# Attention products in four 32-column groups: shapes of the TensorE array, four reciprocals, and a planner that keeps two engines apart

## The chip, the core and the metric

The kernel runs on one core of a Trainium2 chip. Five engines work side by side there: TensorE (PE in the profile; its weight loads are PEld), VectorE (DVE), ScalarE (ACT), GpSimd (POOL) and SyncE (SP), which issues the transfers. Each works through its own list of instructions in order and waits on semaphores for the others. The metric is the device time of one execution in microseconds (us), as the median of several runs. Before the change it is 1353.37 us, the median of 3 runs (1352.94 to 1354.53).

## The reference

Three layers follow each other. The first is a linear attention over 4 batches, 8 heads, 576 positions of 64 numbers, with 128 features:

```python
def phi(x):
    proj = np.einsum('bhsd,df->bhsf', x, w_phi)
    proj = proj - np.max(np.abs(proj), axis=-1, keepdims=True)
    return np.concatenate([np.exp(proj), np.exp(-proj)], axis=-1)
q_p, k_p = (phi(q), phi(k))
kv = np.einsum('bhsf,bhsd->bhfd', k_p, v)
z = np.sum(k_p, axis=2)
num = np.einsum('bhsf,bhfd->bhsd', q_p, kv)
den = np.einsum('bhsf,bhf->bhs', q_p, z)[..., None] + 1e-06
return (num / den).astype(np.float32)
```

Its output, as 2304 tokens of 512 numbers, goes through a feed-forward layer (`x @ w_in`, a leaky activation with a slope for each of 2048 channels, `@ w_out`), and then through four experts of 1024 channels, whose outputs are added with normalised weights.

## The kernel before

Two heads make a pair, so there are 16 pairs. For each pair the attention stage does the following steps. Their names are those of the planner's operations, and the lines are those of the kernel before.

- `P` (L349) projects the keys, then the queries, into five PSUM banks that are handed out in turn (`bank`). A product has 64 rows, so two heads run in two row groups of the array. `PT` (L356) projects the last 64 positions.
- `R` and `S` (L365, L371) on DVE take the largest magnitude and subtract it. `E` and `X` on ACT make the exponentials.
- `KV` (L392) multiplies values and exponentials of the keys: weights of 64 columns, two heads in two column groups. `ZZ` (L401) sums the keys by products with ones, in four column groups of 32. `Z` (L413) adds halves of the keys ahead of it, on DVE or POOL.
- `TV` (L425, L427) turns the result, `T` (L440, L437) transposes the shifted queries.
- `A` (L458, function `attend`) makes the numerators: weights of 64 columns, one column group for each head, with the two halves of the positions in two calls (c = 0, 1). `AD` (L468, `denominators`) makes the denominators in four column groups of 32, one for each head and half.
- `I` (L479 to L486, `invert`) on DVE turns the denominators over, takes eight reciprocals of 32 partitions and spreads them out. `X0`, `X1`, `X2` multiply, round, and take the rest, which gives the feed-forward layer its input in two parts (`Xh`, `Xl`).

Beside it the first feed-forward weights are unpacked (`W`, steps L195 to L201 on DVE, L588 and L595 on DVE or POOL), and blocks of 12 feed-forward products (`U`, L239; `M`, L260) are put between the pairs. When the stage is done, the second stage (the rest of the feed-forward layer) and the experts follow in the order in which they are written.

A product's groups of rows and columns set the shape of the array: row groups (`row`), two column groups (`col`), four column groups (`quarter`), or the whole array (`full`, and `rounded` for the feed-forward products).

Inside the attention stage the order is that of a planner, the class `Plan`. It knows the cost of each operation on each engine that may do it, what must be done before, and how many buffers a ring has. Step by step it picks the operation that can begin first. Among those that begin alike, the lower rank goes first: a number from the table `RANK` plus the pair's number, with `STAY` added where PE would have to change its shape. Each engine then runs its list in that order.

Of the kernel before, what the change touches and what calls it, by code (L numbers as in the profile page):

```python
# [19 lines left out]
P = 128  # L20
B, H, S, D, F = 4, 8, 576, 64, 128
NP = H // 2
NT = B * S
DM = H * D
# [25 lines left out]
RANK = dict(  # L50
    ld=14.86, Pt=-7.2, PT=-11.04, Pk=-11.49, Pq=-3.94, E=17.62, Z=-30.21, KV=-2.39, TV=-18.36, Q=-14.5,
    A=-0.06, F=16.1, W=40.35, U=12.87, G=4.84,
)
# [5 lines left out]
class Plan:  # L59
# [7 lines left out]
    SWITCH = 100  # L67
    STAY = 0.57

    def __init__(self):  # L70
        self.ops, self.bufs, self.readers, self.begun, self.modes = {}, {}, {}, set(), {}

    def op(self, name, costs, after, rank, emit, alloc=(), reads=(), behind=(), late=0, mode=None):
        self.ops[name] = (costs, after, rank, emit, alloc, {*after, *behind}, late)
        self.modes[name] = mode
        for x in reads:
            self.readers.setdefault(x, []).append(name)

    def run(self):
# [23 lines left out]
        def turn(name, e):  # L103
            return self.SWITCH if e == "t" and self.modes[name] != mode[0] else 0

        while ready:
            found = []
            for name in ready:
                t = room(name)
                if t < np.inf:  # L110
                    costs, rank = self.ops[name][0], self.ops[name][2]
                    begin = lambda e: max(t, free.get(e, self.START))
                    e = min(costs, key=lambda e: begin(e) + costs[e] + BIAS.get(e, 0))
                    found.append((begin(e), rank + self.STAY * (turn(name, e) > 0), order[name], name, e))
# [35 lines left out]
def fused(ctx: ExitStack, tc: tile.TileContext, qT, kT, v_main, v_tail, w_phi, alpha, probs, w64, wup, wdn, out):  # L150
# [134 lines left out]
    with ExitStack() as st1:  # L285
# [164 lines left out]
        def attend(p, c):  # L450
# [4 lines left out]
            for s in range(2):  # L455
                for h in range(2):
                    r = slice(h * D, (h + 1) * D)
                    nc.tensor.matmul(nd[r, :HS], tl["kvt", p][:, s * P + h * D:s * P + (h + 1) * D],  # L458
                                     tl["qe", p][:, h, s, c * HS:(c + 1) * HS], start=s == 0, stop=s == 1,
                                     tile_position=(0, h * D), skip_group_check=True)  # L460

        def denominators(p):
            nd = new("bank", ("d", p))
            for s in range(2):
                for h in range(2):
                    for c in range(2):
                        r = 32 * (2 * h + c)
                        nc.tensor.matmul(nd[r:r + 32, :HS], tl["kvt", p][:, 2 * P + s * D + h * 32:2 * P + s * D + (h + 1) * 32],  # L468
# [6 lines left out]
        def invert(p):  # L475
# [24 lines left out]
        for p in range(len(pairs)):  # L500
            for n in "kq":
# [4 lines left out]
            op(("PT", p), {"t": pe32(F, 2)}, [("ld", n, p) for n in "kq"], RANK["PT"] + p, alloc=[("bank", ("t", p))],  # L506
               reads=[(n + "r", p) for n in "kq"], mode="col", emit=lambda e, p=p: project_tails(p))
            for key in [(n, p, h) for n in "kq" for h in range(2)] + [("t", p)]:
# [7 lines left out]
            for h in range(2):  # L516
# [5 lines left out]
            kes = [("ke", (p, h)) for h in range(2)]  # L522
            op(("KV", p, 0), {"t": pe32(2 * F, 2)}, [*es, ("ld", "v", p)], RANK["KV"] + p, alloc=[("kv", p)], mode="col",
               emit=lambda e, p=p: key_values(p, 0))
            op(("KV", p, 1), {"t": pe32(2 * F, 3)}, [("KV", p, 0), ("E", p, 2)], RANK["KV"] + p + 0.1, reads=[*kes, ("ket", p), ("v", p), ("vt", p)],
               mode="col", emit=lambda e, p=p: key_values(p, 1))
            zs = []
            if p >= NZ:
                zs = [("Z", p, h) for h in range(2)]
                for h in range(2):  # L530
                    op(("Z", p, h), lo_cost(512), [("E", p, h)], RANK["Z"] + p, alloc=[("zsum", (p, h))],
                       reads=[("ke", (p, h))], emit=lambda e, a=(p, h): sum_keys(*a, e))
# [19 lines left out]
            for c in range(2):  # L552
                pr_ = RANK["A"] + p + 0.1 * c
                op(("A", p, c), {"t": pe32(HS, 2)}, [*xs[:2 + c], ("VH", p)], pr_, reads=[("qe", p), ("kvt", p)], behind=[("A", p, 0)] * c,
                   alloc=[("bank", ("n", p, c))] + [("num", p)] * (c == 0), mode="col",
                   emit=lambda e, a=(p, c): attend(*a))
# [4 lines left out]
            pr_ = RANK["F"] + p  # L561
            op(("I", p), {"v": 370 + 200 + 8 * 80 + 700}, [("AD", p)], pr_, alloc=[("di", p), ("dt", p), ("dj", p), ("rb", p)],
               reads=[("bank", ("d", p)), ("dt", p), ("di", p), ("dj", p)], emit=lambda e, p=p: invert(p))
            op(("X0", p), lo_cost(S), [("I", p)] + [("N", p, c) for c in range(2)], pr_, reads=[("rb", p)],
               emit=lambda e, p=p: x_part(p, 0, e))
            op(("X1", p), hi_cost(S), [("X0", p)], pr_, emit=lambda e, p=p: x_part(p, 1, e))
            op(("X2", p), lo_cost(S), [("X1", p)], pr_, reads=[("num", p)], emit=lambda e, p=p: x_part(p, 2, e))

# [29 lines left out]
        for i, (c, half) in enumerate(early):  # L598
# [5 lines left out]
            for k, cost in costs.items():  # L604
                op(("W", k, c, half), cost, before, RANK["W"] + WSTEP * i,
                   alloc=[("area", i)] * (k == 0), reads=[("area", i)] * (k == 5), late=4200 * (k == 0),
# [18 lines left out]
        for blk in range(NA):  # L625
            tok = sum(BLOCKS[blk])
            have = [("X2", p) for p, (b, j) in enumerate(pairs) if b * S < tok]
            for cs in (tuple(range(GRP)),):
                for c in cs:
# [7 lines left out]
                       emit=lambda e, a=g: g_step(*a, 0, e))  # L637
                    op(("G1", *g), hi_cost(BLK), [("G0", *g)], pr_, emit=lambda e, a=g: g_step(*a, 1, e))
                    op(("G2", *g), lo_cost(BLK), [("G1", *g)], pr_, alloc=[("gl", g)], reads=[("t", g)],
                       emit=lambda e, a=g: g_step(*a, 2, e))  # L640
# [352 lines left out]
```

## Time and profile before

| What | Value |
|---|---|
| Median of 3 runs | 1353.37 us |
| The profiled execution | 1352.19 us |
| Its span in the trace | 1350.2 us |
| PE busy in the span | 1331.8 us (99%), 7616 matmul records |
| DVE busy | 776.5 us (58%) |
| ACT busy | 443.3 us (33%) |
| POOL busy | 256.9 us (19%) |

The attention stage, with the planner's order, takes about the first 270 us of the span. A product of 32-bit numbers shows as two records, so the four products of one call of `attend` are eight records. Records of PE overlap in the profile, and their ends are modelled. Time on PE is therefore read from start to start here.

### The profile page before, as it was taken

The page shows a single profiled execution, that of the slowest core. Times are in us where ns is not written, and L with a number is a line of the kernel's source. Part 1 is how long each engine was busy: PE and PEld are TensorE (multiplying, and loading weights), DVE is VectorE, ACT ScalarE, POOL GpSimd, SP SyncE. Part 2 cuts the span into 40 slices and gives each one's busy share as a digit, 9 for nine tenths or more (in the row PEclk, how much of TensorE's full clock was granted, in tenths as well). Part 3 has the DMA queues.
Part 4 walks back from the last instruction along what each step waited for, and adds up shares of the span by engine and source line. Part 5 has one row for each costly group of instructions (what it writes and reads, how often), then busy time and mean ns, then how long its engine had stood idle before and what let it go on. Part 6 is the DMA issues. An engine that isn't in the chain of part 4 may idle for free.

```text
span 1350.2 us, 20101 instructions
## 1 busy us (share of the span) xinstructions
PE 1331.8 (99%) x7616; PEld 1130.8 (84%) x7616; DVE 776.5 (58%) x1365; ACT 443.3 (33%) x943; POOL 256.9 (19%) x268
## 2 busy tenths in 40 slices
PE   8899999999999999999999999999999999999998
PEld 5566667788888888898899998998999998899997
DVE  7898766699779555665455446443333363343332
ACT  5655654233122121144444443222222232222221
POOL 1244323012011030056566640000000000000000
PEclk9999999999999999999999999999999999999999
DMA  5222220123102011048877755665566666555641
GB/s 179 85 86 70 63 62 11 48 94 94 48 27 68 0 62 64 0 172 293 296 262 257 252 216 181 225 194 188 188 192 194 197 221 201 172 171 181 192 142 47
DMA packets 103487, 192.27 MB, mean 142 GB/s; under 512 B 13920, under 2 KB 14048, under 8 KB 103392
## 3 DMA queue, kind: packets, MB, share of 16 engines
q1 hardware_dynamic: 103392, 191.00, 43.1%
q8 instruction: 60, 0.98, 0.3%
q14 instruction: 35, 0.29, 0.1%
HBM read 140.10 MB, written 50.86 MB: 141 GB/s over the span
## 4 chain that ended last, share of the span: by engine, by line
PE 89%; DVE 7%; DMA 2%; ACT 1%; issue 1%; SPq 0%; POOL 0%; DVEq 0%; ACTq 0%; POOLq 0%
PE dn L901 29%; PE up L854 25%; PE up L239 12%; PE dn L260 12%; PE mm L260 2%; PE kv L392 2%; PE bank L458 1%; PE bank L349 1%; DVE m L365 1%; PE bank L468 1%; DVE dj L485 1%; PE mm L239 1%; PE kv L401 1%; PE bank L440 1%; DVE pmk L371 1%
## 5 line engine op out<-in xcount | busy, mean ns | idle before, releaser
L901 PE MATMUL dn<-whd,Xh 128*128 128x512 f32 x720 | 231.4, 390 | 0.0
L912 DVE SCALAR_TENSOR_TENSOR acc<-dn,pr,acc 128x512 f32<-128x512 f32 x126 | 88.7, 749 | 190.9 <-PE dn L901 190.9
L854 PE MATMUL up<-Xl,wlu 128*128 128x384 f32 x864 | 158.6, 335 | 0.8 <-DVE c L867 0.6
L901 PEld LDWEIGHTS dn<-whd,Xh 128*128 128x128 f32 x720 | 135.1, 188 | 27.0
L867 DVE TENSOR_TENSOR c<-up,p 128x384 f32<-128x384 f32 x96 | 53.5, 557 | 174.2 <-PE up L854 174.2
L854 PEld LDWEIGHTS up<-Xl,wlu 128*128 128x128 f32 x864 | 150.3, 188 | 2.0 <-DVE c L867 1.5
L901 PE MATMUL dn<-Xh 128*128 128x512 f32 x648 | 151.8, 389 | 0.0
L901 PEld LDWEIGHTS dn<-Xh 128*128 128x128 f32 x648 | 121.6, 188 | 25.5
L901 PE MATMUL dn<-wld,Xh 128*128 128x512 f32 x360 | 140.8, 391 | 0.0
L872 ACT COPY p<-up 128x384 f32<-128x384 f32 x48 | 23.1, 481 | 326.6 <-PE up L854 326.6
L854 PE MATMUL up<-Xl,whu 128*128 128x384 f32 x576 | 111.8, 334 | 1.2 <-ACT p L872 1.2
L854 PEld LDWEIGHTS up<-Xl,whu 128*128 128x128 f32 x576 | 101.2, 188 | 1.5 <-ACT p L872 1.5
L861 ACT ACTIVATE Xh<-c 128x384 fp32r<-128x384 f32 x144 | 75.7, 526 | 79.7 <-DVE c L867 79.7
L239 PE MATMUL up<-Xl,whu 128*128 128x512 f32 (+1 forms) x272 | 99.1, 364 | 0.0
L260 PE MATMUL dn<-gh,wld 128*128 128x512 f32 (+1 forms) x272 | 99.1, 364 | 0.0
L260 PE MATMUL dn<-gh,whd 128*128 128x512 f32 (+1 forms) x272 | 99.1, 364 | 0.0
L239 PE MATMUL up<-Xh,whu 128*128 128x512 f32 (+1 forms) x272 | 99.1, 364 | 0.0
L239 PE MATMUL up<-Xh,wlu 128*128 128x512 f32 (+1 forms) x272 | 99.0, 364 | 0.0
L260 PE MATMUL dn<-gl,whd 128*128 128x512 f32 (+1 forms) x272 | 99.0, 364 | 0.0
L862 DVE SCALAR_TENSOR_TENSOR Xh<-c,Xh 128x384 fp32r<-128x384 f32 x144 | 86.1, 600 | 5.4
L184 ACT CAST gh<-t 128x512 fp32r<-128x512 f32 (+1 forms) x68 | 38.6, 569 | 147.7 <-DVE t L251 147.7
L901 PEld LDWEIGHTS dn<-wld,Xh 128*128 128x128 f32 x360 | 67.5, 188 | 13.1
(172 smaller groups left out, 2226.6 us busy)
## 6 DMA issues: line engine op xcount, KB each, us to landing
whu<-wsu SPq DMA_DIRECT2D x96, 256.0 KB, 3.4
wlu<-wsu SPq DMA_DIRECT2D x96, 256.0 KB, 3.2
st<-w SPq DMA_DIRECT2D x24, 512.0 KB, 3.4
wsu<-whu SPq DMA_DIRECT2D x48, 256.0 KB, 3.1
wsu<-wlu SPq DMA_DIRECT2D x48, 256.0 KB, 3.0
Xh<-wsd SPq DMA_DIRECT2D x48, 256.0 KB, 3.8
wld<-wsd SPq DMA_DIRECT2D x40, 256.0 KB, 3.0
whd<-wsd SPq DMA_DIRECT2D x40, 256.0 KB, 3.3
```

The lines of the kernel that those rows point to most:

```text
L184: nc.scalar.copy(hi, src)
L239: nc.tensor.matmul(ps[:, :bn], a[:, cs], x[:, cc, t0:t0 + bn], start=n == 0, stop=n == 3 * CC - 1)
L260: nc.tensor.matmul(ps, w[:, sl], g, start=start and k == 0, stop=stop and k == 2)
L349: nc.tensor.matmul(ps[h][:, i], x[r, i * P:(i + 1) * P], w0[r, h], start=True, stop=True, tile_position=(h * D, 0), skip_group_check=True)
L392: nc.tensor.matmul(kv[h * D:(h + 1) * D, 0], a, e, start=i == 0, stop=i == NM, tile_position=(0, h * D), skip_group_check=True)
L854: nc.tensor.matmul(ps[name], w[k][:, r, kt * P:(kt + 1) * P], slots[k][:, x + kt], start=start and n == 0, stop=stop and n == 5, skip_grou ...
L861: nc.scalar.activation(gh, src, AF.Relu)
L862: nc.vector.scalar_tensor_tensor(gl, src, 0.0, f32(gh), ALU.max, ALU.subtract)
L867: nc.vector.tensor_tensor(o, ps[name], x, ALU.add)
L872: nc.scalar.copy(p1, ps["pb"])
L901: nc.tensor.matmul(ps[m], x[:, sl], w, start=c == chunks[0] and k == 0, stop=c == chunks[-1] and k == 2)
L912: nc.vector.scalar_tensor_tensor(av, ps[m], pe, av, ALU.mult, ALU.add)
```

## The change

- `PT`, `KV` and `A` are cut into products of 32 columns, four groups at once. `A` and `AD` order the 128 output rows by the half of the head first and by the head second, and the rows of the feed-forward weight `w_in` are put in the same order ahead of the launch. With that order, one reciprocal serves both heads, so `invert` issues four of 64 partitions.
- The planner counts a change of shape twice where the new shape is the whole array, and none between `full` and `rounded`. It no longer lets an operation of POOL run beside one of those of DVE that are marked `port`. Its costs of a feed-forward product and of `I`, `STAY` and the table `RANK` have other values.

```diff
-    STAY = 0.57
+    STAY = 0.98
 ...
         def turn(name, e):
-            return self.SWITCH if e == "t" and self.modes[name] != mode[0] else 0
+            new, old = self.modes[name], mode[0]
+            if e != "t" or new == old or {new, old} == {"full", "rounded"}:
+                return 0
+            return self.SWITCH * (2 if new in ("full", "rounded") else 1)
...
-                    begin = lambda e: max(t, free.get(e, self.START))
+                    port = lambda e: e == "p" or e == "v" and name in self.ports
+                    begin = lambda e: max(t, free.get(e, self.START), free.get("port", 0) if port(e) else 0)
...
+            if e == "p" or e == "v" and name in self.ports:
+                free["port"] = start + cost
...
-        pe = lambda n, k=1: k * (n / 2.4 + 3)
+        pe = lambda n, k=1: k * (n / 2.4 + 13)
...
-                for h in range(2):
-                    nc.tensor.matmul(ps[h * TL:(h + 1) * TL, i * F:(i + 1) * F], tl[n + "r", p][:, NM * P:], w0[:, h],
-                                     start=True, stop=True, tile_position=(0, h * TL), skip_group_check=True)
+                for o in range(0, P, 32):
+                    nc.tensor.matmul(ps[o:o + 32, i * F:(i + 1) * F], tl[n + "r", p][:, NM * P + o % TL:NM * P + o % TL + 32], w0[:, o // TL],
+                                     start=True, stop=True, tile_position=(0, o), skip_group_check=True)
...
-                    nc.tensor.matmul(kv[h * D:(h + 1) * D, 0], a, e, start=i == 0, stop=i == NM,
-                                     tile_position=(0, h * D), skip_group_check=True)
+                    for o in range(0, D, 32):
+                        nc.tensor.matmul(kv[h * D + o:h * D + o + 32, 0], a[:, o:o + 32], e, start=i == 0, stop=i == NM,
+                                         tile_position=(0, h * D + o), skip_group_check=True)
...
-                for h in range(2):
-                    r = slice(h * D, (h + 1) * D)
-                    nc.tensor.matmul(nd[r, :HS], tl["kvt", p][:, s * P + h * D:s * P + (h + 1) * D],
+                for o in range(0, P, 32):
+                    to, h = divmod(o // 32, 2)
+                    a = s * P + h * D + to * 32
+                    nc.tensor.matmul(nd[o:o + 32, :HS], tl["kvt", p][:, a:a + 32],
                                      tl["qe", p][:, h, s, c * HS:(c + 1) * HS], start=s == 0, stop=s == 1,
-                                     tile_position=(0, h * D), skip_group_check=True)
+                                     tile_position=(0, o), skip_group_check=True)
...
-                        r = 32 * (2 * h + c)
+                        r = 32 * (2 * c + h)
...
-            for h in range(2):
-                for c in range(2):
-                    for to in range(2):
-                        a, o = (32 * (2 * h + x) for x in (c, to))
-                        nc.vector.reciprocal(dj[o:o + 32, c * n:(c + 1) * n], di[a:a + 32])
+            for c in range(2):
+                for to in range(2):
+                    nc.vector.reciprocal(dj[to * D:(to + 1) * D, c * n:(c + 1) * n], di[c * D:(c + 1) * D])
...
-    w64 = a(np.stack(chunks(moe_w_in, moe_w_out), axis=1)).view(np.int64)
+    rows = moe_w_in.reshape(CC, 2, 2, 32, DFF).transpose(0, 2, 1, 3, 4).reshape(DM, DFF)
+    w64 = a(np.stack(chunks(rows, moe_w_out), axis=1)).view(np.int64)
```

The operations marked `port` are `Z`, `X0`, `X1`, `X2`, all steps of `W`, `G1` and `G2` (the rounding of a feed-forward result and its rest). Of the table of ranks two entries show the kind: `Pq` goes from -3.94 to -12.68 and `E` from 17.62 to 9.59.

Two places in the order show what moves. The first is PE in a steady pair, behind a block of feed-forward products, from the transposes of pair 10 or the numerators ahead of them to the key sums (`bank` is PSUM, `pmq` and `pmt` the shifted queries, `kr` and `qr` keys and queries as loaded, `ke` the exponentials, `kvt` the turned key-values). Before:

```order
L458 MATMUL bank<-qe,kvt 64x288 x4
L440 MATMUL bank<-ident,pmq 128x128 x8
L437 MATMUL bank<-ident,pmt 128x128
L356 MATMUL bank<-w_122,kr 64x128 x2
L356 MATMUL bank<-w_122,qr 64x128 x2
L392 MATMUL kv<-ke,v 64x256 x4
L458 MATMUL bank<-qe,kvt 64x288 x4
L392 MATMUL kv<-ke,v 64x256 x4
L392 MATMUL kv<-ket,vt_209 64x256 x2
L468 MATMUL bank<-qe,kvt 32x288 x8
L401 MATMUL kv<-zsum,ones 32x256 x4
L401 MATMUL kv<-ket,ones 32x256 x2
```

After:

```order
L449 MATMUL bank<-ident,pmq 128x128 x4
L446 MATMUL bank<-ident,pmt 128x128
L449 MATMUL bank<-ident,pmq 128x128 x4
L364 MATMUL bank<-w_122,kr 32x128 x4
L364 MATMUL bank<-w_122,qr 32x128 x4
L468 MATMUL bank<-qe,kvt 32x288 x8
L401 MATMUL kv<-ke,v 32x256 x8
L468 MATMUL bank<-qe,kvt 32x288 x8
L401 MATMUL kv<-ke,v 32x256 x8
L401 MATMUL kv<-ket,vt_209 32x256 x4
L478 MATMUL bank<-qe,kvt 32x288 x8
L410 MATMUL kv<-zsum,ones 32x256 x4
```

The first numerators have moved from ahead of the transposes to behind them, and all products from the tails' projection to the key sums have the same shape.

The second place is DVE behind the inversion of pair 1 (`dj` takes the reciprocals, `acc_a` here holds weights that are being unpacked, `m` takes the largest magnitudes, `pmt` and `pmk` the shifted tails and keys). Before:

```order
L485 RECIPROCAL dj<-di 32x9 x8
L486 STREAM_TRANSPOSE rb<-dj 128x576
L365 TENSOR_REDUCE m<-bank 128x2
L195 TENSOR_SCALAR acc_a<-acc_a 128x512
L371 TENSOR_TENSOR pmt<-bank,m 128x256
L197 SCALAR_TENSOR_TENSOR acc_a<-acc_a 128x512
L195 TENSOR_SCALAR acc_a<-acc_a 128x512
L365 TENSOR_REDUCE m<-bank 128x4 x2
```

After:

```order
L493 RECIPROCAL dj<-di 64x9 x4
L494 STREAM_TRANSPOSE rb<-dj 128x576
L373 TENSOR_REDUCE m<-bank 128x2
L379 TENSOR_TENSOR pmt<-bank,m 128x256
L203 TENSOR_SCALAR acc_a<-acc_a 128x512
L373 TENSOR_REDUCE m<-bank 128x4 x2
```

Four reciprocals are gone, and of the three steps on weights one is left ahead of the next pair's keys.

## Rows read from the trace of the kernel before

**Rows 1.** Busy time by stretch: us, busy of each engine (x instructions), clock, DMA.
```profile
34.92:124.37 89.45, 81.60 (x763) 54.74 (x763) 82.22 (x166) 52.01 (x123) 36.29 (x27) 0.96 0.29 84
124.37:193.69 69.32, 69.32 (x658) 47.64 (x656) 49.33 (x114) 39.41 (x94) 21.90 (x17) 1.00 0.23 66
193.69:269.70 76.01, 75.30 (x515) 53.87 (x514) 49.56 (x105) 30.22 (x65) 15.96 (x12) 1.00 0.10 30
```

**Rows 2.** Timeline of PE, a steady pair: start us, us, engine, line, operation, x records.
```profile
126.85 1.14 PE L458 MATMUL bank<-qe,kvt 128*64 128x288 f32 x8
127.82 1.03 PE L392 MATMUL kv<-ke,v 128*64 128x256 f32 x8
128.68 0.60 PE L392 MATMUL kv<-ket,vt 128*64 128x256 f32 x4
129.22 1.18 PE L468 MATMUL bank<-qe,kvt 128*32 128x288 f32 x16
130.21 0.61 PE L401 MATMUL kv<-zsum,ones 128*32 128x256 f32 x8
130.64 0.60 PE L401 MATMUL kv<-ket,ones 128*32 128x256 f32 x4
...
134.12 0.50 PE L260 MATMUL mm<-gh,whd 128*128 128x512 f32 x1
134.45 0.40 PE L260 MATMUL mm<-gh,wld 128*128 128x512 f32 x1
...
136.79 0.39 PE L260 MATMUL mm<-gl,whd 128*128 128x512 f32 x1
137.11 1.19 PE L458 MATMUL bank<-qe,kvt 128*64 128x288 f32 x8
138.23 1.09 PE L440 MATMUL bank<-ident,pmq 128*128 128x128 f32 x8
...
139.36 0.44 PE L356 MATMUL bank<-w,kr 128*64 128x128 f32 x4
...
139.85 1.03 PE L392 MATMUL kv<-ke,v 128*64 128x256 f32 x8
```

**Rows 3.** Timeline of PE where transposes follow a feed-forward block.
```profile
208.78 0.40 PE L239 MATMUL mm<-Xh,wlu 128*128 128x512 f32 x1
209.02 1.03 PE L440 MATMUL bank<-ident,pmq 128*128 128x128 f32 x8
```

**Rows 4.** Timeline of DVE in the same steady pair.
```profile
130.46 0.48 DVE L479 STREAM_TRANSPOSE dt<-bank 128x288 f32<-128x288 f32 x1 [2.26 <-PE bank L468]
130.98 0.17 DVE L480 TENSOR_SCALAR di<-dt 128x9 f32<-128x9 f32 x1
131.19 1.74 DVE L485 RECIPROCAL dj<-di 32x9 f32<-32x9 f32 x8
...
137.29 1.27 DVE L371 TENSOR_TENSOR pmq<-bank,m 128x512 f32<-128x512 f32 x2
```

**Rows 5.** Waits of PE from 34.92 to 124.37: us in total, times, longest.
```profile
PE bank L440 <- DVE pmq L371: 4.6, 4, 2.1
```

**Rows 6.** Timelines of DVE and POOL: mask and shift alone, and a shift beside POOL.
```profile
19.52 0.42 DVE L199 TENSOR_SCALAR acc_a<-acc_a 128x512 uint32<-128x512 uint32 x1
19.85 0.42 DVE L195 TENSOR_SCALAR acc_a<-acc_a 128x512 uint32<-128x512 uint32 x1
...
38.86 1.60 DVE L195 TENSOR_SCALAR acc_a<-acc_a 128x512 uint32<-128x512 uint32 x1
...
38.77 1.41 POOL L493 TENSOR_TENSOR num<-num,rb 128x576 f32<-128x576 f32 x1 [3.13 <-DVE rb L486]
```

**Rows 7.** Groups of DVE from 34.92 to 124.37: busy us, mean ns, idle before.
```profile
L195 DVE TENSOR_SCALAR acc_a<-acc_a 128x512 uint32<-128x512 uint32 x6 | 7.2, 1194 | 0.0
L199 DVE TENSOR_SCALAR acc_a<-acc_a 128x512 uint32<-128x512 uint32 x6 | 4.2, 698 | 0.0
```

More of the change, by code (lines that the diff above doesn't have):

```diff
@@ L50 @@
 RANK = dict(
-    ld=14.86, Pt=-7.2, PT=-11.04, Pk=-11.49, Pq=-3.94, E=17.62, Z=-30.21, KV=-2.39, TV=-18.36, Q=-14.5,
-    A=-0.06, F=16.1, W=40.35, U=12.87, G=4.84,
+    ld=13.91, Pt=-8.51, PT=-13.98, Pk=-14.23, Pq=-12.68, E=9.59, Z=-28.15, KV=-2.2, TV=-19.55, Q=-16.92,
+    A=-1.24, F=21.58, W=46.91, U=12.28, G=4.18,
 )
@@ L67, with op @@
     SWITCH = 100
-    STAY = 0.57
+    STAY = 0.98
     def __init__(self):
-        self.ops, self.bufs, self.readers, self.begun, self.modes = {}, {}, {}, set(), {}
-    def op(self, name, costs, after, rank, emit, alloc=(), reads=(), behind=(), late=0, mode=None):
+        self.ops, self.bufs, self.readers, self.begun, self.modes, self.ports = {}, {}, {}, set(), {}, set()
+    def op(self, name, costs, after, rank, emit, alloc=(), reads=(), behind=(), late=0, mode=None, port=False):
         self.ops[name] = (costs, after, rank, emit, alloc, {*after, *behind}, late)
         self.modes[name] = mode
+        if port:
+            self.ports.add(name)
         for x in reads:
@@ L506, in fused @@
             op(("PT", p), {"t": pe32(F, 2)}, [("ld", n, p) for n in "kq"], RANK["PT"] + p, alloc=[("bank", ("t", p))],
-               reads=[(n + "r", p) for n in "kq"], mode="col", emit=lambda e, p=p: project_tails(p))
+               reads=[(n + "r", p) for n in "kq"], mode="quarter", emit=lambda e, p=p: project_tails(p))
             for key in [(n, p, h) for n in "kq" for h in range(2)] + [("t", p)]:
@@ L522, in fused @@
             kes = [("ke", (p, h)) for h in range(2)]
-            op(("KV", p, 0), {"t": pe32(2 * F, 2)}, [*es, ("ld", "v", p)], RANK["KV"] + p, alloc=[("kv", p)], mode="col",
+            op(("KV", p, 0), {"t": pe32(2 * F, 2)}, [*es, ("ld", "v", p)], RANK["KV"] + p, alloc=[("kv", p)], mode="quarter",
                emit=lambda e, p=p: key_values(p, 0))
             op(("KV", p, 1), {"t": pe32(2 * F, 3)}, [("KV", p, 0), ("E", p, 2)], RANK["KV"] + p + 0.1, reads=[*kes, ("ket", p), ("v", p), ("vt", p)],
-               mode="col", emit=lambda e, p=p: key_values(p, 1))
+               mode="quarter", emit=lambda e, p=p: key_values(p, 1))
             zs = []
@@ L530, in fused @@
                 for h in range(2):
-                    op(("Z", p, h), lo_cost(512), [("E", p, h)], RANK["Z"] + p, alloc=[("zsum", (p, h))],
+                    op(("Z", p, h), lo_cost(512), [("E", p, h)], RANK["Z"] + p, port=True, alloc=[("zsum", (p, h))],
                        reads=[("ke", (p, h))], emit=lambda e, a=(p, h): sum_keys(*a, e))
@@ L554, in fused @@
                 op(("A", p, c), {"t": pe32(HS, 2)}, [*xs[:2 + c], ("VH", p)], pr_, reads=[("qe", p), ("kvt", p)], behind=[("A", p, 0)] * c,
-                   alloc=[("bank", ("n", p, c))] + [("num", p)] * (c == 0), mode="col",
+                   alloc=[("bank", ("n", p, c))] + [("num", p)] * (c == 0), mode="quarter",
                    emit=lambda e, a=(p, c): attend(*a))
@@ L561, in fused @@
             pr_ = RANK["F"] + p
-            op(("I", p), {"v": 370 + 200 + 8 * 80 + 700}, [("AD", p)], pr_, alloc=[("di", p), ("dt", p), ("dj", p), ("rb", p)],
+            op(("I", p), {"v": 370 + 170 + 4 * 200 + 700}, [("AD", p)], pr_, alloc=[("di", p), ("dt", p), ("dj", p), ("rb", p)],
                reads=[("bank", ("d", p)), ("dt", p), ("di", p), ("dj", p)], emit=lambda e, p=p: invert(p))
-            op(("X0", p), lo_cost(S), [("I", p)] + [("N", p, c) for c in range(2)], pr_, reads=[("rb", p)],
+            op(("X0", p), lo_cost(S), [("I", p)] + [("N", p, c) for c in range(2)], pr_, port=True, reads=[("rb", p)],
                emit=lambda e, p=p: x_part(p, 0, e))
-            op(("X1", p), hi_cost(S), [("X0", p)], pr_, emit=lambda e, p=p: x_part(p, 1, e))
-            op(("X2", p), lo_cost(S), [("X1", p)], pr_, reads=[("num", p)], emit=lambda e, p=p: x_part(p, 2, e))
+            op(("X1", p), hi_cost(S), [("X0", p)], pr_, port=True, emit=lambda e, p=p: x_part(p, 1, e))
+            op(("X2", p), lo_cost(S), [("X1", p)], pr_, port=True, reads=[("num", p)], emit=lambda e, p=p: x_part(p, 2, e))
         areas = []
@@ L604, in fused @@
             for k, cost in costs.items():
-                op(("W", k, c, half), cost, before, RANK["W"] + WSTEP * i,
+                op(("W", k, c, half), cost, before, RANK["W"] + WSTEP * i, port=True,
                    alloc=[("area", i)] * (k == 0), reads=[("area", i)] * (k == 5), late=4200 * (k == 0),
@@ L637, in fused @@
                        emit=lambda e, a=g: g_step(*a, 0, e))
-                    op(("G1", *g), hi_cost(BLK), [("G0", *g)], pr_, emit=lambda e, a=g: g_step(*a, 1, e))
-                    op(("G2", *g), lo_cost(BLK), [("G1", *g)], pr_, alloc=[("gl", g)], reads=[("t", g)],
+                    op(("G1", *g), hi_cost(BLK), [("G0", *g)], pr_, port=True, emit=lambda e, a=g: g_step(*a, 1, e))
+                    op(("G2", *g), lo_cost(BLK), [("G1", *g)], pr_, port=True, alloc=[("gl", g)], reads=[("t", g)],
                        emit=lambda e, a=g: g_step(*a, 2, e))
```

## The prediction

> **What bounds the kernel now.** I read the page first, then the busy times by stretch, then the timelines of PE and DVE in the attention stage. By the page PE is busy nearly all of the span, so time is won only where PE itself gets shorter or stops waiting. The change touches the attention stage alone: from the first product of the second stage on (at about 270 us of the span), the order of PE's instructions is the same before and after, and PE had no gap there that the change reaches. In the attention stage there are three stretches, which I bound by the starts of the query transposes of pairs 2, 8 and 13 [rows 1]. Up to pair 8 (124.37 us) PE and DVE hold each other up: 81.60 and 82.22 us busy of 89.45. Behind it PE is busy all the time (69.32 of 69.32) and DVE 49.33.
>
> In the full stretch each pair takes 13.86 us on PE (the transposes of pair 8 start at 124.37, of pair 9 at 138.23), and every piece can be read off the starts [rows 2]. Eight records of the numerators (two groups of 64 columns) take 0.97 us from 126.85 to 127.82. Sixteen records of the denominators (four groups of 32 columns) take 0.99, from 129.22 to 130.21. So four groups take the time of two, with twice the records. Each change of tile shape adds time twice. The last piece before it ends late: four records to 129.22 take 0.54, where eight take 0.86, so 0.11. A feed-forward record takes 0.234 (ten from 134.45 to 136.79), but 0.32 from 136.79 to 137.11, so 0.09. And the first record behind it is slow: 0.33 instead of 0.23 at 134.12, and the numerators at 137.11 take 1.12 instead of 0.97, of which 0.10 are the change behind them and 0.05 the first set. I take 0.15 a change: 0.10 of drain and 0.02 (four groups) to 0.10 (128-wide weights) of slow start, 0.05 in the middle. Between a feed-forward product and a full transpose there is none: 0.24 from 208.78 to 209.02 [rows 3].
>
> **Part 1, the shapes.** With all column products in four groups, the order has 85 changes of shape in place of 127 in the attention stage: 20 to 15 up to the transposes of pair 2, 44 to 31 up to pair 8, 40 to 25 up to pair 13, 21 to 13 behind. In a steady pair 8 become 5: gone are feed-forward to numerators (0.09 + 0.05), numerators to transposes (0.10 + 0.06) and key-values to denominators (0.11 + 0.02); the one into the projection of tails loses 0.03. That is 0.46 us a pair.
>
> The products double: the records of the projection of tails, key-values and numerators grow by 704 (44 a pair). For numerators the row of the denominators is the very form, so +0.02 per pair and half is the upper end, and nothing the lower. For key-values, eight zsum records in four groups take 0.43 (130.21 to the next piece, half of the 0.86 of eight records in two groups), again nothing. The projection of tails has no such row: 128 columns wide, it would start a record every 0.027 us, and the closest that is shown is 0.054. Bounds: nothing, or twice its time, 0.44 a pair (0.49 from 139.36 to 139.85 less 0.05 of slow start), 7 us over 16 pairs. I take nothing, since its weight columns per set stay 128 as before; the 7 us stay in the range.
>
> The Trainium skill, TensorEngine Tiling (Array Packing), section Instruction Overhead, says that every matmul carries about 60 cycles and that one should not take a tiling factor from a dimension that is already small. By that rule, unhidden, 704 records would cost an estimated 17.6 us and the change would lose. The trace disagrees for sets that run side by side: sixteen records in the time of eight.
>
> **Part 2, four reciprocals.** Eight take 1.74 us [rows 4], 0.217 each. Each new one has 64 partitions and the same 9 elements; the scalar addition on 128 partitions and 9 elements takes 0.17, so partitions don't cost, and four save 0.87 a pair on DVE. If they took twice as long nothing would be saved. Where DVE is not waited for, that is hidden under PE.
>
> **Part 3, what is late next in a steady pair.** The removal of the numerators between feed-forward and transposes takes away the cover of the query subtraction. Before: the chain on DVE starts 0.25 us behind the denominators (130.46), and the first query subtraction ends at 137.29 + 0.68 = 137.97; transposes start at 138.23, when PE comes to them. After: from the start of the next piece on PE (130.21) the feed-forward product ends 0.09 before 137.11, at 137.02, so 6.81 behind. DVE comes to 137.97 - 0.87 = 137.10, and with 0.1 that I allow for the signal PE starts at 137.20. PE then waits 0.2 a pair. In sum a steady pair goes from 13.86 to 13.60, 0.26 less; it is DVE's latency that sets it, not PE. Five steps (pairs 8 to 13) give 1.3 us.
>
> **Part 4, the stretch where DVE is late (34.92 to 124.37).** PE waits there for query subtractions, 4.6 us in four waits [rows 5]. Six inversions lose 0.87 each, 5.2. The order also keeps DVE's SBUF operations and POOL apart. Alone, the shift of a weight chunk takes 0.42 and the mask 0.42; with POOL's product of 38.77 running, a shift that starts at 38.86 takes 1.60, until POOL is done [rows 6]. Six shifts of mean 1194 ns lose 4.6, six masks of mean 698 lose 1.7 [rows 7]: 6.3 to be had, if the order meets its aim; others of that kind I leave uncounted, against those that will still meet. DVE's 82.22 would become 70.7. PE's own floor is 81.60 less 13 changes (2.0) and less what the lower clock took (0.96 of 89.45, 3.6 us; the low level may come back or not): 76 to 79.6. Before, the two engines handed work to each other over five PSUM banks and ended 8 us above the busier one. With both lower I take 81, nearer to the floor than to 89.45, since DVE now has 10 us of slack: 8.4 us won. The ends are 4 and 13.
>
> **Ahead and behind.** Up to pair 2: one inversion in DVE's chain (0.87) and five changes, 1.6 us. Behind pair 13: eight changes, 1.2 us. The sum is 1.6 + 8.4 + 1.3 + 1.2 = 12.5. The second stage starts earlier by that and runs as before: the same PE order, and DVE's different mix of weight preparation there lies under a busy PE (if it were late, about 1 us). The profiled execution took 1352.19, so 1339.7; the median is 1.18 above that execution: 1340.9.
>
> **The rivals.**
> - Shapes alone: DVE's relief reaches no one, because ScalarE's exponentials, the banks and the order in which they come free hold the early stretch. For it: copies of ScalarE stand behind exponentials there. Against it: PE's waits name DVE. 42 changes at 0.15 give 6.3: 1347.
> - The steady pair waits more: the wait in front of the transposes is 0.7 and not 0.2, as DVE starts later or POOL's sums hold it. Nine steps by 0.5 cost 4.5: 1345. Against it: DVE idles before the inversion (the rows of DVE begin with a wait on PE).
> - Slower: the four weight loads of a set are not hidden under the set that runs. Then each set pays the slow first set, 0.05. Sets: 4 of tails, 10 of key-values, 8 of numerators a pair, 352 in all, 17.6 us, and 1340.9 + 17.6 = 1358.5. It decides from 0.036 a set (12.5 / 352). Against it stands the row of denominators, whose later sets pay nothing.
> - No effect: the early stretch gets new waits that eat the switches too: 1353.
>
> **The numbers.** Forecast (1336 to 1345) 0.60, shapes alone 0.17, longer wait 0.10, no effect 0.07, slower 0.06. Range 1335 to 1350: the low end is the stretch at its floor of 76 with everything else as forecast (1335.9), the high end takes in shapes alone with part of the tails' 7 us. 0.2% (2.7 us) is what a measurement can tell from no change; faster 0.87, same 0.07, slower 0.06.
>
> **What would show it.** After: numerators and key-values in sets of four at 0.97 and 0.86; a steady pair of 13.5 to 13.7 with PE waiting about 0.2 for the query subtraction; four reciprocals in 0.87; shifts of weights near 0.42; pair 8's transposes at 113 to 116 us and not 124.37; the second stage from about 257. Wrong if blocks of four groups are longer than those of two, if shifts stay at 1.2, or if pair 8 comes after 120.

## The result, and the profile after

The changed kernel takes 1337.49 us (median of 4 runs, 1337.3 to 1338.27), where the kernel before takes 1353.63 beside it (median of 4). The ratio is 0.9881, with a 95% interval of 0.9864 to 0.9899: faster by 1.2%. The forecast was 1340.9 in a range of 1335 to 1350. So the direction is as forecast and the time lies in the range, 3.4 us below the value.

The head of the page of the changed kernel:

```profile
span 1335.5 us, 21458 instructions
PE 1324.3 (99%) x8320; PEld 1127.6 (84%) x8320; DVE 758.6 (57%) x1306; ACT 444.5 (33%) x946; POOL 245.1 (18%) x260
```

The span fell by 14.7 (1350.2 to 1335.5). The busy time of PE fell by only 7.5 (1331.8 to 1324.3), though it has 704 records more: half of the gain is idle time that PE lost, and half is shorter work.

The busy times by stretch, bounded as before by the query transposes of pairs 2, 8 and 13, and by the first product of the second stage (us, then busy us and instructions of each engine, granted clock, DMA share, GB/s). They answer to [rows 1]:

```profile
33.33:110.87 77.54, 75.86 (x1002) 51.94 (x1003) 72.95 (x147) 52.26 (x123) 26.62 (x20) 1.00 0.32 98
110.87:179.25 68.38, 68.02 (x875) 47.40 (x876) 44.71 (x93) 40.02 (x96) 21.81 (x17) 1.00 0.24 67
179.25:253.36 74.11, 73.91 (x653) 53.92 (x654) 46.64 (x91) 31.01 (x67) 12.87 (x10) 1.00 0.10 31
```

The second stage and the experts follow from 253.36 to the end of the span. By subtraction from these bounds and those of [rows 1]:

| Stretch | Before | After | Difference | Forecast |
|---|---|---|---|---|
| up to the transposes of pair 2 | 34.92 | 33.33 | -1.6 | -1.6 |
| pair 2 to pair 8 | 89.45 | 77.54 | -11.9 | -8.4 |
| pair 8 to pair 13 | 69.32 | 68.38 | -0.9 | -1.3 |
| pair 13 to the second stage | 76.01 | 74.11 | -1.9 | -1.2 |
| second stage and experts | 1080.5 | 1082.1 | +1.6 | 0 |
| sum | 1350.2 | 1335.5 | -14.7 | -12.5 |

The timeline of PE in a steady pair answers to [rows 2] (start us, us, engine, line, operation, records):

```profile
128.92 1.05 PE L401 MATMUL kv<-ke,v 128*32 128x256 f32 x16
129.78 0.61 PE L401 MATMUL kv<-ket,vt 128*32 128x256 f32 x8
130.21 1.15 PE L478 MATMUL bank<-qe,kvt 128*32 128x288 f32 x16
131.18 0.61 PE L410 MATMUL kv<-zsum,ones 128*32 128x256 f32 x8
...
137.53 0.39 PE L268 MATMUL mm<-gh,wld 128*128 128x512 f32 x1
137.77 0.40 PE L268 MATMUL mm<-gl,whd 128*128 128x512 f32 x1
138.23 0.63 PE L449 MATMUL bank<-ident,pmq 128*128 128x128 f32 x4
...
139.33 0.43 PE L364 MATMUL bank<-w,kr 128*32 128x128 f32 x8
139.57 0.40 PE L364 MATMUL bank<-w,qr 128*32 128x128 f32 x8
139.79 1.15 PE L468 MATMUL bank<-qe,kvt 128*32 128x288 f32 x16
140.76 1.05 PE L401 MATMUL kv<-ke,v 128*32 128x256 f32 x16
```

From start to start, sixteen records of the numerators take 0.97 (139.79 to 140.76) and sixteen of the key-values 0.86 (128.92 to 129.78), as eight did. The projections of tails take 0.24 and 0.22 (from 139.33 and 139.57), where two groups of 64 took 0.49 for both. The change of shape between key-values and denominators is gone: eight records to 130.21 take 0.43. The one gap left is in front of the transposes: a feed-forward record takes 0.24 (137.53 to 137.77), and the last one 0.46 (137.77 to 138.23).

The timeline of DVE in the same pair answers to [rows 4]:

```profile
131.43 0.48 DVE L489 STREAM_TRANSPOSE dt<-bank 128x288 f32<-128x288 f32 x1 [4.18 <-PE bank L478]
...
132.16 0.87 DVE L493 RECIPROCAL dj<-di 64x9 f32<-64x9 f32 x4
...
137.40 1.27 DVE L379 TENSOR_TENSOR pmq<-bank,m 128x512 f32<-128x512 f32 x2
```

Four reciprocals of 64 partitions take 0.87, half of the eight. The first query subtraction ends at about 138.08 (137.40 and, as before, 0.68), 0.15 before the transposes start. That they wait for DVE is an inference here; the third experiment tests it.

The waits of PE between pairs 2 and 8, whole (waited for: us in total, times, longest), answer to [rows 5]:

```profile
PE bank L449 <- ACT ke L384: 0.9, 1, 0.9
PE bank L449 <- DVE pmq L379: 0.3, 1, 0.3
PE bank L468 <- DVE pmk L379: 0.2, 1, 0.2
```

The 4.6 us of waiting for query subtractions are 0.3 now. And the groups of DVE that unpack weights there (records, busy us, mean ns of one, idle before) answer to [rows 7]; L203 is the shift and L207 the mask:

```profile
L203 DVE TENSOR_SCALAR acc_a<-acc_a 128x512 uint32<-128x512 uint32 x6 | 4.0, 661 | 0.0
L596 DVE TENSOR_TENSOR acc_a<-acc_a 128x512 f32<-128x512 f32 x5 | 3.4, 682 | 0.0
L207 DVE TENSOR_SCALAR acc_a<-acc_a 128x512 uint32<-128x512 uint32 x6 | 2.5, 418 | 0.1
```

A mask takes 418 ns, which is its time alone [rows 6]; a shift takes 661 on average, down from 1194, so some still meet POOL.

### The profile page after: what moved, and what is told of

Same layout as the page of the kernel before. It is cut to its first block, busy times and chain, and to the rows that moved or that the text cites. A ratio compares the mean times of both kernels' runs of the same rounds, so it can differ in the third digit from the quotient of the medians.

```text
span 1335.5 us, 21458 instructions
## 1 busy us (share of the span) xinstructions
PE 1324.3 (99%) x8320; PEld 1127.6 (84%) x8320; DVE 758.6 (57%) x1306; ACT 444.5 (33%) x946; POOL 245.1 (18%) x260
## 4 chain that ended last, share of the span: by engine, by line
PE 89%; DVE 7%; DMA 1%; ACT 1%; issue 1%; SPq 0%; POOL 0%; DVEq 0%; ACTq 0%; POOLq 0%
PE dn L909 29%; PE up L862 26%; PE dn L268 11%; PE up L247 11%; PE mm L268 3%; PE mm L247 2%; PE bank L468 2%; PE kv L401 2%; PE bank L357 1%; DVE m L373 1%; PE bank L478 1%; PE bank L449 1%; PE kv L410 1%; DMA acc_a<-w 0%; DVE pmk L379 0%
## 5 line engine op out<-in xcount | busy, mean ns | idle before, releaser
L870 DVE SCALAR_TENSOR_TENSOR Xh<-c,Xh 128x384 fp32r<-128x384 f32 x144 | 85.4, 594 | 5.5
```

The costliest lines, as they stand in the source:

```text
L870: nc.vector.scalar_tensor_tensor(gl, src, 0.0, f32(gh), ALU.max, ALU.subtract)
```

## The experiments

Each ran beside the kernel before on the same chip (medians of 15 runs: 1352.44 us for the first four, 1352.02 for the others). The theory to be tested: the early stretch (pair 2 to pair 8) ends with DVE's work, so that whatever DVE loses there comes off the time; behind it only changes of shape and the wait in front of the transposes count. The stretches are those of one profiled execution each. All diffs are against the changed kernel, and shortened.

| Kernel | Median us | Ratio to before (95%) | Pair 2 to 8 | 8 to 13 | 13 to second stage |
|---|---|---|---|---|---|
| shapes, before's order | 1351.03 | 0.9991 (0.9982 to 1.0) | 89.3 | 68.5 | 75.7 |
| the same, four reciprocals | 1346.66 | 0.9951 (0.9939 to 0.9964) | 86.4 | 68.5 | 73.8 |
| after, eight reciprocals | 1347.84 | 0.9959 (0.9945 to 0.9973) | 82.3 | 72.7 | 76.8 |
| after, no port rule | 1347.33 | 0.9958 (0.9945 to 0.9972) | 85.4 | 68.4 | 74.5 |
| after again | 1337.84 | 0.9895 (0.9882 to 0.9909) | 77.5 | 68.4 | 74.1 |
| after, inversion split | 1332.57 | 0.9858 (0.9845 to 0.9872) | 76.9 | 67.2 | 73.7 |
| after's order, two groups, eight reciprocals | 1349.49 | 0.9983 (0.9974 to 0.9991) | 82.5 | 73.5 | 77.2 |
| after, eight in the last pair | 1336.69 | 0.9885 (0.987 to 0.9901) | 77.5 | 68.4 | 74.2 |

**Shapes alone.** The planner, its ranks, its costs and what it takes for the operations' shapes are those of before, and with them the order. The products have four groups, and the reciprocals are eight:

```diff
-            for c in range(2): for to in range(2):
-                nc.vector.reciprocal(dj[to * D:(to + 1) * D, ...], di[c * D:(c + 1) * D])
+            for c in range(2): for to in range(2): for h in range(2):
+                nc.vector.reciprocal(dj[o:o + 32, ...], di[r:r + 32])
```

> Planner, table of ranks and order of the kernel before; all column products in four groups of 32; eight reciprocals. Theory (four groups take the time of two, and only the changes of shape count): 127 changes become 110, 17 by 0.12 us, so about 2 us less than before (1351 to 1352). Rival (more records or unhidden weight loads cost): not less than before, up to 17 us more. In the trace numerators and key-values would be 0.97 and 0.86 us by the theory, longer by the rival.

Measured: 1351.03, 1.4 us below before. A steady pair takes 13.71 in place of 13.86, which is the one change that goes without a new order (key-values to denominators, 0.12) and the slow first set of the tails (0.03). The early stretch stays:

```profile
34.81:124.08 89.27, 79.20 (x1019) 52.23 (x1019) 82.50 (x166) 51.76 (x123) 36.27 (x27) 0.98 0.28 85
```

PE is busy for 2.4 less than in [rows 1], in part by a clock of 0.98 and not 0.96, yet the stretch loses 0.2. So PE's own work doesn't set its end, and DVE (82.50 here, 82.22 before) did not change. The shapes bring little by themselves, and they cost nothing: the rival of unhidden weight loads (17.6 us) is out.

**Shapes and four reciprocals.** The kernel above, with the four reciprocals of the change.

> As e1_shapes, with four reciprocals of 64 partitions for eight of 32. Theory (DVE's chain sets the early stretch): six or seven inversions of 0.87 us go from the chain, 4 to 6 us less than e1_shapes (about 1346), all of it ahead of pair 8's transposes; behind, the steady pair keeps its time, since PE is the later one there in the old order. Rival (reciprocals are hidden): same as e1_shapes within 1 us.

Measured: 1346.66, 4.4 less than with eight.

```profile
33.50:119.91 86.41, 78.70 (x1023) 52.35 (x1019) 78.35 (x143) 51.48 (x122) 36.76 (x27) 0.98 0.28 88
```

DVE lost 4.15, the stretch 2.86: most of it comes through, though not one to one. The steady pairs did not change (68.50 in both): with before's order the chain on DVE has cover there. Not all of the gain lies ahead of pair 8, as was expected: 1.3 come off ahead of pair 2 (34.81 to 33.50) and 1.9 behind pair 13, while the second stage and the experts lose 2.6.

**After with eight reciprocals.** The changed kernel, with the eight reciprocals of the first diff; its planner still plans for four.

> The changed kernel with eight reciprocals of 32 partitions in the place of four; the planner's costs and so the order as in the changed kernel. Theory (in the new order DVE's chain ends last in front of the transposes of every pair): each steady pair longer by 0.87 us (13.68 to about 14.5), 12 to 13 us over 15 inversions, 1349 to 1350. Rival (DVE has slack behind pair 8, so reciprocals count only ahead of it): 5 us, about 1342.

Measured: 1347.84; its span is 11.0 above that of the changed kernel. 12 to 13 were expected: the attention stage gets 13.6 longer, and what follows it 2.6 shorter (see the second stage below).

```profile
35.20:117.50 82.30, 76.08 (x1002) 51.92 (x1003) 77.80 (x171) 52.12 (x123) 26.61 (x20) 1.00 0.30 92
117.50:190.20 72.70, 67.98 (x875) 47.40 (x876) 48.75 (x113) 39.84 (x96) 21.81 (x17) 1.00 0.22 63
```

In the first row PE has the work of the changed kernel (76.08 and 75.86), DVE 4.85 more, and the stretch is 4.76 longer: what DVE gets there comes out nearly one to one. In the second row PE is idle for 4.7. The timeline of PE shows where:

```profile
145.26 0.39 PE L268 MATMUL mm<-gl,whd 128*128 128x512 f32 x1
146.58 0.63 PE L449 MATMUL bank<-ident,pmq 128*128 128x128 f32 x4 [0.93 <-DVE pmq L379]
...
151.81 0.61 PE L401 MATMUL kv<-ket,vt 128*32 128x256 f32 x8
152.24 1.15 PE L478 MATMUL bank<-qe,kvt 128*32 128x288 f32 x16
```

The last feed-forward record and the wait behind it take 1.32 (145.26 to 146.58), 0.86 more than the 0.46 of the changed kernel, and a pair takes 14.54 in place of 13.68. That is the 0.87 of the four reciprocals within a hundredth. It shows that in the new order the DVE chain from the denominators to the query subtraction is the last to end in a steady pair, and that behind pair 8 this order loses time without the four reciprocals: 72.7, where before's order with the same products and eight took 68.5.

**After without the port rule.** The planner lets DVE's SBUF steps and POOL run at the same time again:

```diff
-        if port:
-            self.ports.add(name)
...
-            if e == "p" or e == "v" and name in self.ports:
+            if False:
                 free["port"] = start + cost
```

> The changed kernel with no port rule in its planner: POOL and DVE operations may be put beside each other; shapes, reciprocals, table and costs as in the changed kernel. The order of PE stays but for one place. Theory (the rule is worth what the DVE operations no longer wait): shifts and masks of weights wait for POOL again, 3 to 5 us more, 1341 to 1343, all of it ahead of pair 8. Rival (the table of ranks and the earlier denominators do it, the rule is nothing): within 1 us of the changed kernel.

Measured: 1347.33, 9 to 10 above the changed kernel, where 3 to 5 were expected. The profiled execution is its fastest (1346.05); in it the early stretch is 7.8 longer than with the rule.

```profile
33.59:118.95 85.36, 76.11 (x1003) 51.10 (x1003) 79.89 (x143) 51.03 (x121) 34.05 (x25) 1.00 0.28 89
```

PE's work is the same again; DVE is busy for 6.9 more with four records fewer, so its records got longer. Its groups (L201 is the shift, L205 the mask in this kernel):

```profile
L201 DVE TENSOR_SCALAR acc_a<-acc_a 128x512 uint32<-128x512 uint32 x6 | 6.0, 997 | 0.0
L205 DVE TENSOR_SCALAR acc_a<-acc_a 128x512 uint32<-128x512 uint32 x6 | 5.7, 954 | 0.0
L594 DVE TENSOR_TENSOR acc_a<-acc_a 128x512 f32<-128x512 f32 x2 | 3.4, 1682 | 0.1
```

and the timelines of DVE, then of POOL, at one such place:

```profile
47.57 1.38 DVE L205 TENSOR_SCALAR acc_a<-acc_a 128x512 uint32<-128x512 uint32 x1
48.99 0.69 DVE L207 SCALAR_TENSOR_TENSOR acc_a<-acc_a 128x512 f32<-128x512 uint32 x1
49.72 1.65 DVE L594 TENSOR_TENSOR acc_a<-acc_a 128x512 f32<-128x512 f32 x1
...
47.40 1.28 POOL L594 TENSOR_TENSOR acc_a<-acc_a 128x512 f32<-128x512 f32 x1 [7.02 <-DVE acc_a L207]
49.41 1.42 POOL L601 TENSOR_TENSOR wld<-acc_a,whd 128x512 fp32r<-128x512 f32 x1 [0.73 <-ACT whd L161]
```

The mask of 47.57 ends at 48.95, behind POOL's 48.68. The record of 48.99 starts between two steps of POOL and takes 0.69. That of 49.72 takes 1.65 and ends at 51.37, behind POOL's 50.83; without POOL this step takes 0.68. So a weight step of DVE that starts beside a running POOL step lasts until that step is done. That does not hold for every step on SBUF. The four reciprocals of another pair ran beside a POOL step and took what they take alone:

```profile
98.87 0.88 DVE L491 RECIPROCAL dj<-di 64x9 f32<-64x9 f32 x4
...
98.76 1.27 POOL L601 TENSOR_TENSOR wld<-acc_a,whd 128x512 fp32r<-128x512 f32 x1
```

A step that the planner gave to POOL to relieve DVE (1.28 to 1.42) held DVE up for longer (0.96 and 0.97) than doing it would have taken (0.68). Without the rule the new order, with its four reciprocals, is no better than before's order with the same products (1346.66). No run has the rule with before's table of ranks, so how much of the 7.8 needs the new table is not shown.

**After with the inversion split.** The DVE chain is last in the steady pairs, and its last step, the transpose that spreads the reciprocals (0.78), is needed by no query. This edit makes it an operation of its own, planned behind the query subtraction of the pair two further on:

```diff
+LATE = 5
+        def spread(p):
+            nc.vector.transpose(rb..., dj.to_broadcast([P, S // 32, 32]))
...
+            op(("B", p), {"v": 700}, [("I", p)], pr_, alloc=[("rb", p)],
+               behind=[("S", "q", p + 2, 1)] * (LATE <= p < len(pairs) - 2), ...)
```

> The changed kernel with the last transpose of an inversion as an operation of its own, which from pair 5 on comes behind the next pair's query subtractions. Theory (in a steady pair PE waits 0.23 us for DVE's chain, and PE's own time is next): the chain gets up to 0.6 us shorter, a steady pair 13.45 us and not 13.68, eight or nine pairs, 2 us less than the changed kernel. Rival (something else sets the steady pair, such as ScalarE's exponentials or the buffers): 13.68 stays, no gain.

Measured: 1332.57, 5.3 below the changed kernel on the same chip. Its timelines of PE and DVE:

```profile
137.21 0.40 PE L269 MATMUL mm<-gl,whd 128*128 128x512 f32 x1
137.44 1.05 PE L450 MATMUL bank<-ident,pmq 128*128 128x128 f32 x8
```

```profile
136.51 1.28 DVE L380 TENSOR_TENSOR pmq<-bank,m 128x512 f32<-128x512 f32 x2
137.70 0.77 DVE L498 STREAM_TRANSPOSE rb<-dj 128x576 f32<-128x576 f32 x1
```

The last feed-forward record takes 0.23 like the others (137.21 to 137.44). The gap is gone, a steady pair takes 13.44 where 13.45 was expected, and between pairs 8 and 13 PE is busy for all of it:

```profile
110.52:177.70 67.18, 67.18 (x876) 47.68 (x876) 49.05 (x98) 39.99 (x95) 14.27 (x12) 1.00 0.23 68
```

Against the changed kernel's second profile the gain is 1.2 in the steady pairs, 0.7 and 0.5 in the stretches beside them, 0.9 ahead of pair 2 and 1.9 in the second stage and the experts. The first of these is what the theory asks for. The two beside it come with the new order that the planner finds, which also takes steps from POOL (12 records and not 17 in the row above), and are not taken apart here. The last two do not come from the shorter chain: ahead of pair 2 the second profile was 1.3 slower than the first, at a lower clock (see "After again"), and 1.7 of the 1.9 are late waits in the second stage (see there) that this version does not have. So of the 5.3 us at most 2.4 are the moved transpose, and 1.2 are shown to be. This version beats both kernels.

**Two groups in after's order.** Products of 64 columns as before, natural order of the heads, eight reciprocals; all else as after. It is to be compared with the third experiment.

```diff
-                for o in range(0, P, 32):
-                    nc.tensor.matmul(nd[o:o + 32, :HS], tl["kvt", p][:, a:a + 32], ...)
+                for h in range(2):
+                    nc.tensor.matmul(nd[r, :HS], tl["kvt", p][:, s * P + h * D:s * P + (h + 1) * D], ...)
```

> Order of the changed kernel on every engine, but the three products in two groups of 64 columns as before, which needs the eight reciprocals of 32 partitions: to be compared with e3_after_eight (eight reciprocals, four groups). The changes of shape become 103 where e3_after_eight has 85. Theory: 18 changes by 0.12 to 0.15 us, 2.2 to 2.7 us more than e3_after_eight (ratio to before about 0.998), the steady pair 14.54 + 0.14. Rival (four groups are worth more than their changes): a steady pair longer by 0.5 us or more.

Measured: 1349.49, 1.7 above the third experiment (2.1 by each one's own kernel before). A steady pair takes 14.69 in place of 14.54. The timeline of PE shows the change of shape that comes back:

```profile
151.76 0.60 PE L400 MATMUL kv<-ket,vt 128*64 128x256 f32 x4
152.29 1.18 PE L476 MATMUL bank<-qe,kvt 128*32 128x288 f32 x16
153.29 0.61 PE L409 MATMUL kv<-zsum,ones 128*32 128x256 f32 x8
```

The tails of the key-values take 0.53 to the next start where four groups took 0.43 (151.81 to 152.24 above), and the denominators behind them 1.00 in place of 0.97. Together 0.13, the price the prediction had taken for this change. So the shapes alone are worth 1.4 us in before's order and about 2 in after's, and the rest of the change makes the time: the reciprocals, which need the new order of the rows, and the planner.

**The second stage.** It has PE's order of before but took 1.6 us longer. The changed kernel's timelines of PE and DVE there:

```profile
325.01 0.39 PE L268 MATMUL dn<-gl,whd 128*128 128x512 f32 x1
325.47 0.50 PE L268 MATMUL dn<-gh,whd 128*128 128x512 f32 x1
325.80 0.40 PE L268 MATMUL dn<-gh,wld 128*128 128x512 f32 x1
326.62 0.50 PE L268 MATMUL dn<-gl,whd 128*128 128x512 f32 x1 [0.42 <-DVE gl L195]
```

```profile
324.62 0.68 DVE L220 TENSOR_TENSOR w<-w,u 128x512 f32<-128x512 f32 x1
...
325.88 0.68 DVE L195 TENSOR_TENSOR gl<-t,gh 128x512 fp32r<-128x512 f32 x1
```

A product that needs `gl` (the rest of a feed-forward result) waits until DVE has done it, here behind a step of unpacking weights (L220). There are four late products (behind the starts at 308.73, 325.01, 325.80 and 331.96). Three wait for `gl`; the one at 325.47 takes `gh`, which ACT rounds from a result that DVE finished just ahead of it. The four take 2.1 us from start to start, where a record takes 0.23, and the record behind each takes 0.33: 1.6 us too much, the whole difference. With eight reciprocals in the last pair alone, DVE's order in the second stage is that of the third experiment, which has none of the four:

```diff
+            if p < len(pairs) - 1:
                 (four reciprocals)
+            else:
+                (eight reciprocals)
```

> The changed kernel with eight reciprocals in the last pair alone. The attention stage keeps its order, and behind it DVE gets the order that e3_after_eight has in the second stage. Theory (the four late waits for the rest of a feed-forward result in the second stage come from DVE's order there): the second stage takes 1079.6 us and not 1082.1, 2 to 2.5 us less than the changed kernel. Rival (they come from the earlier start against the transfers): 1082 stays.

Measured: 1336.69, 1.2 below the changed kernel on the same chip. The four waits are gone. With the experts the second stage took 1080.74, where the changed kernel's two profiles have 1082.13 and 1081.17. The stretch from the first product of the second stage to the first of the experts tells more, in the changed kernel and in this one:

```profile
253.36:584.30 330.94, 330.37 (x1633) 279.99 (x1632) 247.42 (x396) 77.61 (x138) 52.20 (x48) 1.00 0.16 54
254.22:583.50 329.28, 329.28 (x1633) 280.32 (x1632) 246.12 (x396) 77.71 (x138) 52.12 (x48) 1.00 0.16 55
```

It takes 330.94 and 330.86 in the changed kernel's two profiles and 329.28 here, 1.6 to 1.7 less, as the four waits ask for. It is 329.19 in the kernel before and 329.18 in the third experiment, which has DVE's order of this one. With before's order it goes the same way: 329.19 with eight reciprocals (the first experiment), 331.52 with four (the second). So the order that DVE, and ACT with it, has behind the last pair causes these waits. Four reciprocals in the last pair bring the worse order, except with the inversion split (329.19). The experts behind it took 750.0 to 751.5 in all these profiles, and 0.9 apart in two of the same kernel: that part is spread.

**After again.** The changed kernel a second time, for the spread.

> The changed kernel once more, on the chip of the next three, as their measure. Both theories: 0.988 of the kernel before (its interval was 0.9864 to 0.9899).

Measured: 1337.84, ratio 0.9895. The three stretches are those of the first profile within 0.01 us; up to pair 2 it took 1.3 longer, and the second stage with the experts 1.0 less. Up to pair 2 the granted clock was 0.95 here, where the first profile has 1.00, and PE was busy for 31.16 in place of 30.48; PE's wait for a transfer of keys was 1.9 and not 0.9. The kernel with eight reciprocals in the last pair, which has the same order up to there, took 34.12 at a clock of 1.00. So a single execution tells the length of this stretch to about 1 us, and the 1.6 of the first table with it.

## Why the prediction was right, point by point

- **What bounds the kernel.** Right: PE full behind pair 8, PE and DVE holding each other up ahead of it. In the early stretch DVE's work sets the end up to the change: the stretch less DVE's busy time is 7.2 before, 6.8 and 8.1 with before's order, 5.5 without the port rule, 4.5 with eight reciprocals and 4.6 after. In the changed kernel PE is nearer still: it has 1.7 of idle time left there.
- **The shapes (part 1).** Right in kind and size. Sets of four groups run in the time of two, at 0.97 and 0.86. The tails, for which a bound of 7 us was kept, run at 27 ns a record (eight in 0.22), so the value taken, nothing, holds. The estimate of 17.6 us by the Trainium skill (TensorEngine Tiling (Array Packing), section Instruction Overhead) is not borne out: 704 records more made the time 1.4 us shorter in before's order and about 2 shorter in after's.
- **The reciprocals (part 2).** 0.87, as worked out.
- **The wait in a steady pair (part 3).** Right in place and nearly in size: 0.23 where 0.2 was forecast, a pair of 13.68 where 13.60 was. DVE's chain was timed to 0.01 (6.90 from the end of the denominators to the first subtraction, 6.89 forecast); of the 0.08 that the pair is longer, 0.05 is the signal, 0.15 and not the 0.1 that was allowed. It comes in every pair, so the term is 0.9 and not 1.3.
- **The early stretch (part 4): the term that was mis-sized.** 11.9 against 8.4. Its mechanism held, as the third and fourth experiments show: taken back one at a time, the reciprocals are worth 4.8 us (5.2 forecast) and the rule that keeps DVE and POOL apart 7.8 (6.3); the two overlap, so they don't add up. The step that failed is the last: "nearer to the floor than to 89.45", which gave 81. PE's work came to 75.86, the low end of the floor of 76 to 79.6, because the granted clock was 1.00 of the higher level (2.4 GHz) in place of a mean of 0.96. And PE idled for only 1.68 above it; the 81 held 1.4 to 5 us of such waits, with no row behind them. So two of the signs that were named failed: the transposes of pair 8 came at 110.87 and not at 113 to 116, and a shift took 0.66 and not 0.42.
- **Contention left out on the other side.** Three more steps at L596 and three at L603 came to DVE from POOL (POOL 27 to 20 records), some 6 x 0.69 = 4.1 us more work for DVE. From 82.22 to 72.95 DVE lost 9.3; less the 4.8 of the reciprocals, plus these 4.1, the contention taken away is 8 to 9 and not 6.3. Shift and mask gave 4.9 of their 6.3 (11.4 to 6.5 us); the rest comes from other DVE steps, which were left uncounted.
- **Ahead of pair 2.** 1.6, as forecast, but in part by luck. The shapes alone gave 0.1 there and not 0.75. The six profiles with four reciprocals took 33.3 to 34.6, the four with eight 34.7 to 35.2: 1.1 apart by their means, where 0.87 was counted.
- **Behind pair 13.** 1.9 and not 1.2, and from another cause. The shapes alone took 0.4 off (76.01 to 75.65), the four reciprocals 1.9 more (73.79); in after's order 0.5 and 2.6 (77.21, 76.75, 74.11). The term was all shapes, with the reciprocals at nothing. (The stretch's changes are 23 and 14 by the records, nine fewer; the prediction's four counts add up to 125 and 84, not to its 127 and 85.)
- **The second stage.** "Under a busy PE" was wrong, by the 1 us named for that case and more: up to the experts it took 1.7 longer in both executions (330.94 and 330.86, before 329.19).
- **The rivals.** Shapes alone (1347): out, since DVE's relief comes through, 2.9 of 4.15 us with before's order and 4.76 of 4.85 with after's. A longer wait in the steady pair: it is 0.23; with eight reciprocals it would have been 1.1. No effect: out. Slower by weight loads: out. The errors had both signs: 3.5 and 0.7 too little gain, 0.4 and 1.6 too much, which leaves 2.2 on the execution. Another 1.1 is the allowance between the profiled execution and the median: 1.18 was taken, 0.12 measured. That they leave so little is luck in part.

## What to carry to other kernels

Where two engines hand work to each other, look for the one whose lost microsecond comes off the stretch, by adding a known amount to it alone: 4.85 us more on DVE made it 4.76 longer, while 2.4 less on PE, in before's order, gave 0.2. Work given to a helper engine relieves nothing where the one then waits for the other: two steps of 0.68 that went to POOL held DVE up for 0.96 and 0.97. And when an order takes away the cover of a chain, look in that chain for a step that nobody in it needs: moving one transpose of 0.78 took 1.2 us off five steady pairs, where the shapes alone took 0.8.

## What was not expected of the hardware

- A shift, a mask or a sum of two tiles on DVE beside a running POOL step waits for it rather than sharing: 1.38 and 1.65 in place of 0.42 and 0.68, each ending 0.27 and 0.54 behind POOL's step. Four reciprocals beside such a step took 0.88, as alone.
- Products of 32 columns, 128 elements wide, in four column groups start every 27 ns on average (eight in 0.22), with their weight loads hidden.
- PE's clock fell to the lower level (1.2 GHz) for a part of the early stretch in the profiles with before's order (0.96 before, 0.98 in the first two experiments) and not in those with after's (1.00). PE's idle time in sum doesn't decide it: PE idled for 9.3 of 85.36 at 1.00 without the port rule, and for 7.9 of 89.45 at 0.96 before. Nor does the order alone: three of the five executions without the port rule show 0.996 or 0.997 over their whole span, as the kernel before does (0.994 to 0.999), and the changed kernel's second profile shows 0.95 ahead of pair 2. What decides it stays open.
